# A long convolution and a maxout FFN on one core: shorter conversion, sums on another engine, a reordered drain, x loaded ahead of z, and later slots for the convolution's second product

## The chip, the cores and the metric

One core of a Trainium2 chip. The metric is the device time of one launch in microseconds, median of several runs; lower is better. Times are compared by their ratio to the kernel before on the same chip in the same rounds, and all that are quoted here are of the state "fast"; profiles of kernels that ran on different chips are set side by side as well, each a single execution. Within one kernel the runs spread over some 1 to 14 us (the kernel before: 2421.82 to 2435.97 in one set of rounds), so differences of 2 or 3 us are read only with the interval of the ratio.

## The reference, cut to what matters

```python
def _attn_ref(x, v, pos_emb, w1, w2):            # batch 4, sequence 12544, d_model 128
    h_filt = (np.maximum(pos_emb @ w1, 0.0) @ w2) * np.exp(-0.01 * pos)[:, None]
    u = x * v
    Uf = np.fft.rfft(u, n=2 * S, axis=1); Hf = np.fft.rfft(h_filt, n=2 * S, axis=0)
    y = np.fft.irfft(Uf * Hf[None], n=2 * S, axis=1)[:, :S, :]
    return x * y

def _moe_ref(x, w1, w2, w3, w_out):              # 50176 tokens, d_ff 768
    return np.maximum(np.maximum(x @ w1, x @ w2), x @ w3) @ w_out
```

## The kernel before

The transform of length S is split into three stages of matrix products over 45 pairs g of outputs. For each pair TensorE makes a second stage, the spectrum is multiplied with the filter's (two products and a sum on VectorE, a swap of real and imaginary part on ScalarE), TensorE makes the third stage, VectorE, ScalarE and a last pair of sums finish it, and a DMA stores it to `zd`. Batch 0 goes through a loop of its own (140 to about 330 us). The convolutions of batches 1 to 3 run **beside** the FFN of the batch ahead of them: the FFN is a stream of steps (192 to a batch, 12 to a round), and each piece of the convolution has a slot, the step that it is put into.

Names in the lines below: `pa` and `pb` are the two products of an FFN step, `hid` the hidden tile made of them, `ops` the output products; `ps` is what a stage of the transform leaves, `xt` and `xs` the spectrum's two parts, `dt` and `zs` what follows the third stage; `ht` is the filter's spectrum (made as `sps` in batch 0's loop, stored to `hd` and loaded again beside the FFN); `zt` is the convolution's result read back from `zd`, `yps` its last inverse stage, `gt` that times x. An `h_load` loads ht, a `w_load` the transform's weights wt.

```python
    def g_swap(g):   # ScalarE: xs from the second stage's ps
    def g_re(g):     # VectorE: first product  xt <- ps, ht
    def g_im(g):     # VectorE: second product xs <- xs, ht
        nc.vector.tensor_tensor(out=xss[g][:], in0=xss[g][:], in1=hts.pop(g)[:, 1], op=ALU.mult)
    def g_sum(g):    # VectorE: sum            xt <- xt, xs   (both inputs in SBUF)
        nc.vector.tensor_tensor(out=xts[g][:], in0=xts[g][:], in1=xss.pop(g)[:], op=ALU.add)
    def g_third(g):  # TensorE: third stage    ps <- xt, wt
    ...
        for g in range(NK):                       # the slots of the convolution beside the FFN
            s = s0 + int(g * per_pair)            # per_pair about 2.6 steps
            at(s - 5, 0, w_load, g, 0)
            at(s - 4, 0, h_load, g)
            at(s, 0, w_load, g, 1)
            at(s, 1, g_second, g)
            at(s + 1, 0, g_swap, g)
            at(s + 1, 0, g_re, g)
            at(s + 2, 0, g_im, g)
            at(s + 2, 0, g_sum, g)
            at(s + 4, 1, g_third, g)
            at(s + 5, 0, g_over_c, g)
            at(s + 6, 0, g_turn, g)
            at(s + 7, 0, g_pair, g)
            at(s + 8, 0, g_store, b, g)
    ...
    for s in range(-1, NK + 5):                   # batch 0's own loop, cut
        ...
        if 0 <= s - 3 < NK:
            g_pair(s - 3)                         # two sums on GpSimd
            g_store(0, s - 3)                     # GpSimd issues the store to zd
        ...
        if NK <= s < NK + 2:                      # the drain: first stages of batch 1 ...
            for v in range(4):
                u_first(2 * (s - NK) + v // 2, v % 2)
    folded = [fold(0)]                            # ... then the folds of the FFN's linear part
    u_turn(4); u_turn(5)
    ...
    # FFN: one step is pa (4 matmuls), Relu on ScalarE, pb, maximum on VectorE, then the
    # output products of an earlier round; GpSimd makes twelve sums of hidden tiles a round.
```

## Time and profile before

| what | value |
|---|---|
| time, three runs | 2433.48 us (2431.56 to 2436.21) |
| profiled span, granted TensorE clock | 2426.1 us, 0.989 (this execution took 2427.91 us) |
| TensorE busy / idle in the span | 2325.7 / 100.4 us |
| first matmul of the FFN (pa) | 353.9 us |
| from there to the end ("main stage" below) | 2426.1 - 353.9 = 2072.2 us |

TensorE is busy for 96% of the span, so the kernel is bounded by it, and a change that leaves its work alone can only remove its idle time, or time that it spends at a lower clock. The prediction below shows the lines of the stages; two groups of the page that it does not show are needed later. The columns of the page's groups are line, engine, operation, output and inputs, count, then busy time and mean ns of one, then the idle time of the engine just before them and what ended it:

```profile
L131 PE MATMUL ps<-xt,wt 128*64 128x128 f32 x2880 | 191.8, 276 | 15.7 <-DVE xt L430 10.6
L430 DVE TENSOR_TENSOR xt<-xt,xs 128x512 f32<-128x512 f32 x180 | 236.7, 1315 | 6.2
```

The third stages (the 180 pairs' matmuls ps<-xt,wt) waited 10.6 us in all for VectorE's sum. The sum takes 1315 ns in the mean, against the 0.69 us that one takes undisturbed.

### The profile page before, as it was taken

What the parts mean: (1) busy time and instruction counts of PE and PEld (TensorE: products, weight loads), DVE (VectorE), ACT (ScalarE), POOL (GpSimd) and SP (SyncE); (2) the same over time, 40 slices, a digit from 0 to 9 for tenths busy, and PEclk for the clock granted to TensorE, in tenths of its full rate; (3) what the DMA queues carried; (4) which work ended last, traced back from release to release, by engine and by line L of the source; (5) the groups of instructions that cost most, each with busy time, mean ns of one, the idle gap of its engine ahead of it and who ended that gap; (6) DMA issues with size and microseconds to landing.
All of it is one profiled execution on the core that took longest, in us unless ns stands there. A gap on an engine that the chain in (4) does not pass through costs nothing.

```text
span 2426.1 us, 72839 instructions
## 1 busy us (share of the span) xinstructions
PE 2325.7 (96%) x29745; PEld 1630.8 (67%) x29745; DVE 1514.7 (62%) x2801; ACT 1086.8 (45%) x2340; POOL 1586.1 (65%) x1923
## 2 busy tenths in 40 slices
PE   8898879999999999999999999999999999999998
PEld 8787756666666656676666666676666666666665
DVE  5978856657677656657777756657677653333333
ACT  1478745544444435545444434554444432222222
POOL 2879846647766767647677676657777675555555
PEclk9999989999999999999999999999999999999999
DMA  6758859977878739978777749978877752222221
GB/s 152 181 176 269 277 151 178 170 180 207 210 205 221 216 93 174 195 162 230 215 208 219 194 126 186 188 162 208 228 210 219 200 135 63 66 65 52 67 64 21
DMA packets 455223, 408.95 MB, mean 169 GB/s; under 512 B 327132, under 2 KB 331375, under 8 KB 454889
## 3 DMA queue, kind: packets, MB, share of 16 engines
q1 hardware_dynamic: 422240, 315.25, 54.9%
q0 software_dynamic: 32064, 87.60, 11.9%
q8 instruction: 234, 3.83, 0.7%
q10 hardware_dynamic: 585, 1.45, 0.3%
q14 instruction: 100, 0.82, 0.1%
HBM read 295.87 MB, written 84.67 MB: 157 GB/s over the span
## 4 chain that ended last, share of the span: by engine, by line
PE 77%; POOL 8%; DVE 6%; DMA 4%; issue 4%; ACT 1%; SPq 1%; ACTq 0%; POOLq 0%; DVEq 0%
PE ops L607 19%; PE pa L131 19%; PE pb L131 19%; PE ps L131 8%; PE ps L140 6%; PE yps L131 4%; POOL zs L461 3%; DVE xs L427 1%; DVE xt L430 1%; DMA zt<-zd 1%; POOL zd L465 1%; DVE dt L446 1%; POOL hd L806 1%; PE pm L301 1%; DMA wt<-wt_const 1%
## 5 line engine op out<-in xcount | busy, mean ns | idle before, releaser
L558 ACT ACTIVATE hid<-pa 128x392 f32<-128x392 f32 x768 | 382.2, 498 | 785.0 <-PE pa L131 770.2
L561 DVE TENSOR_TENSOR hid<-hid,pb 128x392 f32<-128x392 f32 x768 | 428.5, 559 | 419.6 <-PE pb L131 411.4
L131 PE MATMUL pa<-gt,w_sb 128*64 128x392 f32 x3072 | 640.3, 495 | 0.0
L131 PE MATMUL pb<-gt,w_sb 128*64 128x392 f32 x3072 | 638.2, 494 | 1.5 <-ACT hid L558 1.2
L131 PEld LDWEIGHTS pb<-gt,w_sb 128*64 128x64 f32 x3072 | 220.0, 137 | 291.4 <-issue 266.8
L629 POOL DMA_DIRECT2D out_dram<-o x256 | 162.4, 639 | 333.7 <-DVE o L624 180.6
L607 PE MATMUL ops<-hid,wo_sb 128*64 128x196 f32 x3072 | 331.9, 329 | 16.3 <-DVE hid L561 16.3
L607 PEld LDWEIGHTS ops<-hid,wo_sb 128*64 128x64 f32 x3072 | 218.9, 137 | 157.3 <-issue 115.4
L577 POOL TENSOR_TENSOR s<-hid 128x392 f32<-128x392 f32 x192 | 201.7, 1051 | 158.7 <-DVE hid L561 128.7
L461 POOL TENSOR_TENSOR zs<-dt 128x256 f32<-128x256 f32 x360 | 282.6, 806 | 26.8 <-ACT dt L454 24.6
L577 POOL TENSOR_TENSOR s<-hid,s 128x392 f32<-128x392 f32 x192 | 199.0, 1036 | 104.5 <-DVE hid L561 103.5
L430 DVE TENSOR_TENSOR xt<-xt,xs 128x512 f32<-128x512 f32 x180 | 236.7, 1315 | 6.2
L577 POOL TENSOR_TENSOR hid<-hid,s 128x392 f32<-128x392 f32 x192 | 205.7, 1074 | 48.4 <-DVE hid L561 28.3
L548 DVE TENSOR_TENSOR gt<-yps,xT 128x392 f32<-128x392 f32 x128 | 72.2, 564 | 227.5 <-PE ops L607 173.9
L131 PEld LDWEIGHTS pa<-gt,w_sb 128*64 128x64 f32 x3072 | 198.3, 138 | 16.0 <-issue 2.0
L131 PE MATMUL ps<-xt,wt 128*64 128x128 f32 x2880 | 191.8, 276 | 15.7 <-DVE xt L430 10.6
L131 PE MATMUL ps<-spec,wt 128*64 128x128 f32 x2880 | 191.1, 275 | 14.6 <-DVE dt L446 10.2
L577 POOL TENSOR_TENSOR hid<-hid 128x392 f32<-128x392 f32 x192 | 203.8, 1075 | 0.6
L140 PE MATMUL ps<-f,uT 98*64 98x90 f32 x4096 | 192.2, 245 | 9.2 <-DVE dt L446 4.2
L154 DVE TENSOR_TENSOR spec<-tmp,ps 128x180 f32<-128x180 f32 (+1 forms) x448 | 143.0, 363 | 84.8 <-ACT tmp L152 83.9
L140 PEld LDWEIGHTS ps<-f,uT 98*64 98x64 f32 x4096 | 180.0, 139 | 20.2 <-issue 9.2
L427 DVE TENSOR_TENSOR xs<-xs,ht 128x512 f32<-128x512 f32 x180 | 189.6, 1054 | 0.0
(101 smaller groups left out, 3169.9 us busy)
## 6 DMA issues: line engine op xcount, KB each, us to landing
wt<-wt_const SPq DMA_DIRECT2D x360, 256.0 KB, 5.2
ht<-hd SPq DMA_DIRECT2D x270, 256.0 KB, 4.6
zd<-zs POOLq DMA_DIRECT2D x180, 256.0 KB, 4.4
zt<-zd SPq DMA_DIRECT2D x256, 180.0 KB, 3.9
ut<-in_xr_dram SPq DMA_DIRECT2D x128, 196.0 KB, 3.8
ut<-in_vr_dram SPq DMA_DIRECT2D x128, 196.0 KB, 4.0
xT<-in_x_dram SPq DMA_DIRECT2D x512, 49.0 KB, 3.1
out_dram<-o POOLq DMA_DIRECT2D x256, 98.0 KB, 3.7
```

The lines of the kernel that those rows point to most:

```text
L131: nc.tensor.matmul(out[64 * h:64 * h + 64], lhsT[:, 64 * h:64 * h + 64], rhs, start=start, stop=stop, skip_group_check=True)
L140: nc.tensor.matmul(ps[64 * c:64 * c + 64, 256 * i + r * N1:256 * i + (r + 1) * N1], a[:, r, :], table[:, r, c * N1:(c + 1) * N1], start=(i ...
L154: nc.vector.tensor_tensor(out=dst[:, :, c, :], in0=tmp, in1=v[:, 0], op=op)
L427: nc.vector.tensor_tensor(out=xss[g][:], in0=xss[g][:], in1=hts.pop(g)[:, 1], op=ALU.mult)
L430: nc.vector.tensor_tensor(out=xts[g][:], in0=xts[g][:], in1=xss.pop(g)[:], op=ALU.add)
L461: nc.gpsimd.tensor_tensor(out=zs[:, a], in0=dt[:, 0:2, :], in1=dt[:, 2:4, :], op=op)
L548: nc.vector.tensor_tensor(out=g[:].rearrange("d (w t) (m a) -> d w t m a", w=2, a=2), in0=y, in1=xT.rearrange("d w t (m a) -> d w t m a", ...
L558: nc.scalar.activation(h[:], pa[:, 0:N], Relu)
L561: nc.vector.tensor_tensor(out=h[:], in0=h[:], in1=pb[:, 0:N], op=ALU.max)
L577: nc.gpsimd.tensor_tensor(out=out[:], in0=a[:], in1=b[:], op=op)
L607: nc.tensor.matmul(ps[64 * c:64 * c + 64, 0:H2], w, rhs[:, H2 * c:H2 * c + H2], start=start, stop=True, skip_group_check=True)
L629: nc.gpsimd.dma_start(dst[64 * m:64 * m + 64, 64 * c + 2 * i:64 * c + 2 * i + 4, b, :], t[m][64 * c:64 * c + 64].rearrange("d k (q n) -> d ...
```

## The change

Five parts. (1) The conversion of the FFN's weights from double precision to single takes nine VectorE instructions and one on ScalarE in place of twelve on VectorE. (2) In batch 0's loop the last pair of sums moves from GpSimd to VectorE. (3) In the drain the folds come ahead of the last third stage, and the four first stages of batch 1 that stood there come behind it. (4) x is loaded ahead of z. (5) Beside the FFN, the second product and the sum get a slot one step later, everything behind them moves a step with them, and the load of the filter's spectrum two.

```diff
-            lambda: two(out=f1_, in0=hi, scalar1=12, scalar2=9, ...),
-            lambda: one(f1_, f1_, ONE, op=ALU.bitwise_or),
+            lambda: one(f1_, hi, 0xFFFFF, op=ALU.bitwise_and),
+            lambda: nc.scalar.activation(f1f, f1_, Copy, bias=1 - 2.0 ** -20, scale=2.0 ** -20),
 ... (two more VectorE instructions are merged, one is dropped)
-    def g_pair(g):
+    def g_pair(g, eng=nc.gpsimd):
-            nc.gpsimd.tensor_tensor(out=zs[:, a], ...)
+            eng.tensor_tensor(out=zs[:, a], ...)
 ...
-            at(s - 4, 0, h_load, g)
+            at(s - 2, 0, h_load, g)
 ...
-            at(s + 2, 0, g_im, g)
-            at(s + 2, 0, g_sum, g)
-            at(s + 4, 1, g_third, g)
-            at(s + 5, 0, g_over_c, g)
-            at(s + 6, 0, g_turn, g)
-            at(s + 7, 0, g_pair, g)
-            at(s + 8, 0, g_store, b, g)
+            at(s + 3, 0, g_im, g)
+            at(s + 3, 0, g_sum, g)
+            at(s + 5, 1, g_third, g)
+            at(s + 6, 0, g_over_c, g)
+            at(s + 7, 0, g_turn, g)
+            at(s + 8, 0, g_pair, g)
+            at(s + 9, 0, g_store, b, g)
 ...
     def t_load(b, i):
+        if i % 2 == 0:
+            x_load(b, i)                # the eight loads of x, formerly after zt
         zt = ...
 ...
-            g_pair(s - 3)
+            g_pair(s - 3, nc.vector)
 ...
-        if NK <= s < NK + 2:
+        if s == NK:
+            folded = [fold(0)] ...      # all folds here
+        if NK + 2 <= s < NK + 4:
             for v in range(4):
-                u_first(2 * (s - NK) + v // 2, v % 2)
+                u_first(2 * (s - NK - 2) + v // 2, v % 2)
```

More of the change, by code (lines that the diff above doesn't have):

```diff
@@ L202, in convert @@
                         op0=ALU.logical_shift_right, op1=ALU.bitwise_or),
-            lambda: two(out=f1_, in0=hi, scalar1=12, scalar2=9,
-                        op0=ALU.logical_shift_left, op1=ALU.logical_shift_right),
-            lambda: one(f1_, f1_, ONE, op=ALU.bitwise_or),
+            lambda: one(f1_, hi, 0xFFFFF, op=ALU.bitwise_and),
+            lambda: nc.scalar.activation(f1f, f1_, Copy, bias=1 - 2.0 ** -20, scale=2.0 ** -20),
             lambda: two(out=ex, in0=hi, scalar1=1, scalar2=21,
@@ L209, in convert @@
                         op0=ALU.subtract, op1=ALU.max),
-            lambda: one(ex, ex, 255, op=ALU.min),
-            lambda: one(ex, ex, 23, op=ALU.logical_shift_left),
+            lambda: two(out=ex, in0=ex, scalar1=255, scalar2=1 << 23,
+                        op0=ALU.min, op1=ALU.mult),
             lambda: two(out=sg, in0=hi, scalar1=31, scalar2=31,
@@ L214, in convert @@
             lambda: tt(out=ex, in0=ex, in1=sg, op=ALU.bitwise_or),
-            lambda: one(f1f, f1f, 2.0 ** -20, op=ALU.subtract),
             lambda: nc.vector.scalar_tensor_tensor(
@@ L460, in g_pair @@
         for a, op in enumerate((ALU.add, ALU.subtract)):
-            nc.gpsimd.tensor_tensor(out=zs[:, a], in0=dt[:, 0:2, :], in1=dt[:, 2:4, :], op=op)
+            eng.tensor_tensor(out=zs[:, a], in0=dt[:, 0:2, :], in1=dt[:, 2:4, :], op=op)
         zss[g] = zs
@@ L513, with x_load @@
     zts, xTs, gs = ({} for _ in range(3))
+    def x_load(b, i):
+        xT = hp.tile([D, 2, 4, NB], FP32, tag="xT", name="xT", bufs=2)
+        for w in range(2):
+            for c in range(GC):
+                nc.sync.dma_start(xT[c * NG:(c + 1) * NG, w],
+                                  x[:, 64 * w + 2 * i:64 * w + 2 * i + 4, c, b, :])
+        for n in range(2):
+            xTs[b, i + n] = xT[:, :, 2 * n:2 * n + 2]
     def t_load(b, i):
+        if i % 2 == 0:
+            x_load(b, i)
         zt = hp.tile([N1, 2, 512], FP32, tag="zt", name="zt", bufs=2)
@@ L522, in t_load @@
         zts[b, i] = zt
-        if i % 2:
-            return
-        xT = hp.tile([D, 2, 4, NB], FP32, tag="xT", name="xT", bufs=2)
-        for w in range(2):
-            for c in range(GC):
-                nc.sync.dma_start(xT[c * NG:(c + 1) * NG, w],
-                                  x[:, 64 * w + 2 * i:64 * w + 2 * i + 4, c, b, :])
-        for n in range(2):
-            xTs[b, i + n] = xT[:, :, 2 * n:2 * n + 2]
     def t_last(i):
@@ L848 @@
             u_load(1, loads[s])
-        if NK <= s < NK + 2:
+        if s == NK:
+            folded = [fold(0)]
+            for f in range(1, NF):
+                folded.append(fold(f))
+                folded.pop(0)()
+            folded.pop()()
+        if NK + 2 <= s < NK + 4:
             for v in range(4):
-                u_first(2 * (s - NK) + v // 2, v % 2)
-    folded = [fold(0)]
+                u_first(2 * (s - NK - 2) + v // 2, v % 2)
     u_turn(4)
     u_turn(5)
-    for f in range(1, NF):
-        folded.append(fold(f))
-        folded.pop(0)()
-    folded.pop()()
     nc.scalar.copy(lin[:], pl[:, 0:D])
```

## The prediction

> **What bounds the kernel now.** I read the busy shares and the chain of waits first, to see which engine carries the end.
>
> ```profile
> PE 2325.7 (96%) x29745; PEld 1630.8 (67%) x29745; DVE 1514.7 (62%) x2801; ACT 1086.8 (45%) x2340; POOL 1586.1 (65%) x1923
> ...
> PE 77%; POOL 8%; DVE 6%; DMA 4%; issue 4%; ACT 1%; SPq 1%; ACTq 0%; POOLq 0%; DVEq 0%
> ```
>
> The reader is to see a ceiling: TensorE (PE) is busy 2325.7 of 2426.1 us, and the change removes none of its work, so whatever it does must come out of about 100 us of TensorE's idle time. Next I cut the span into stages by what the code does there, with busy time of each engine.
>
> ```profile
> 0.00:71.00 71.00, 63.42 (x1347) 61.67 (x1347) 37.32 (x85) 17.02 (x24) 16.48 (x32) 0.93 0.70 166
> ...
> 71.00:140.00 69.00, 57.71 (x1086) 52.69 (x1084) 61.47 (x116) 28.45 (x45) 64.66 (x58) 0.95 0.58 136
> ...
> 140.00:330.00 190.00, 161.87 (x3294) 140.66 (x3291) 158.96 (x235) 153.61 (x317) 154.95 (x219) 0.98 0.81 253
> ...
> 330.00:356.00 26.00, 19.10 (x266) 15.45 (x265) 9.31 (x29) 7.78 (x25) 4.26 (x6) 0.76 0.36 93
> ...
> 356.00:1908.00 1552.00, 1513.39 (x18564) 1040.59 (x18562) 1039.68 (x1929) 734.80 (x1617) 1042.39 (x1269) 1.00 0.80 192
> ```
>
> The columns after the length are busy time of PE, weight loads, DVE, ACT, POOL, then granted clock, DMA share and GB/s. Idle TensorE per stage: 8, 11, 28, 7 and 39 us; the last 518 us hold 9. The parts of the change fall one into each of the last four rows, so I took each stage's own chain.
>
> First transforms, 71 to 140: GpSimd runs without a gap, three sums of the filter and one product per round.
>
> ```profile
> 93.14 1.13 POOL L342 TENSOR_TENSOR ut<-ut 128x392 f32<-128x392 f32 x1
> 94.24 1.17 POOL L699 TENSOR_TENSOR specH<-specH 128x384 f32<-128x384 f32 x1
> 95.50 1.17 POOL L700 TENSOR_SCALAR specH<-specH 128x384 f32<-128x384 f32 x1
> 96.75 1.00 POOL L701 TENSOR_TENSOR specH<-specH 128x384 f32<-128x384 f32 x1
> 97.71 1.02 POOL L342 TENSOR_TENSOR ut<-ut 128x392 f32<-128x392 f32 x1
> ```
>
> First loop, 140 to 330: the chain is GpSimd again, the sums of k1 and three DMA issues.
>
> ```profile
> 204.66 1.42 POOL zs L461 x2
> 206.38 0.73 POOL zd L465
> 207.64 0.45 POOL hd L806
> 208.21 2.02 POOL zs L461 x2
> ```
>
> Drain, 321 to 356, on TensorE's timeline: the last third stage waits behind four first stages, then the weights f4p and the loads of zt are waited for.
>
> ```profile
> 330.65 1.95 PE L131 MATMUL ps<-xt,wt 128*64 128x128 f32 x16
> ...
> 347.45 1.80 PE L131 MATMUL yps<-f4p,zt 90*64 90x49 f32 x32 [3.37 <-DMA f4p<-f4p_const]
> 352.14 1.95 PE L131 MATMUL yps<-f4p,zt 90*64 90x49 f32 x32 [2.88 <-DMA zt<-zd]
> ```
>
> Main stage: few waits, some of them long, and each time VectorE was late with a maximum because two SBUF operations had been held up.
>
> ```profile
> PE ops L607 <- DVE hid L561: 16.3, 8, 3.5
> PE ps L131 <- DVE xt L430: 9.9, 14, 1.2
> ```
>
> ```profile
> 1865.55 2.75 DVE L430 TENSOR_TENSOR xt<-xt,xs 128x512 f32<-128x512 f32 x1
> 1868.22 0.55 DVE L561 TENSOR_TENSOR hid<-hid,pb 128x392 f32<-128x392 f32 x1
> ```
>
> **What the Trainium skill says.** "SBUF — State Buffer", § Who interferes with whom: a VectorE instruction with two SBUF inputs, or in a two-port mode, and a GpSimd instruction that reads SBUF exclude each other for a whole instruction. The trace agrees: xt<-xt,xs takes 0.69 us when GpSimd is quiet, 1.10, 2.08 or 2.75 us beside it. "GPSIMD Engine Reference", § 3.1: an fp32 sum is about twice as slow there as on VectorE; here 128x256 sums average 884 ns on GpSimd up to 420 us, while VectorE's 128x384 two-SBUF sums repeat every 0.48 us. "DMA: Bandwidth & Descriptors", § Specifications: about 358 GB/s of HBM per core. The trace shows less: 267 GB/s at a share of 0.86, and at most 277 in any slice. "TensorE: Matmul & The Clock Gate", § What's actually happening: an idle window halves the clock. The trace agrees in part: after the 2.62 us wait at 1868 us the next pa group takes 1.52 instead of 0.83 us, though not after every such wait.
>
> **The change part by part.**
>
> Conversion. A job of twelve VectorE instructions becomes nine and one on ScalarE; eight jobs go from 96 steps to 80. By the counts in the code 58 steps are issued before the transforms of u begin and four per round after it, so conversion ends after 22/4 = 5.5 rounds instead of 38/4 = 9.5. VectorE is not the limit there; the gain is GpSimd's. Thirteen rounds of GpSimd, from the sum at 69.60 to that at 132.09, take 62.5 us. The last two, free of conversion, take 4.28 each. The eleven before take 53.9, of which 1.4 are the wait for and issue of the last raw load at 83.9 (0.57 + 0.82), so 4.78 each. After: 6 x 4.78 + 7 x 4.28 = 58.6 us, the raw load being issued earlier in an idle gap. Gain 4 us, all on the path. ScalarE's added copy (about 0.5 us, from its 0.46 us copies of 360 columns) is hidden: it is busy 28 of 69 us.
>
> Sums of k1. Per iteration GpSimd has 2 sums (1.42 to 2.02 us the pair), 0.73 for the zd issue, 1.08 for two hd issues and gaps; zd issues are 47.0 us apart over 12 iterations (202.83 to 249.83), so 3.92 us. Without the sums it needs about 2 us. What is next? TensorE: 0.44 + 1.03 + 1.90 = 3.37. ScalarE: 3.98 between its rounds (203.43 to 207.41) less 0.56 idle = 3.42. VectorE: dt 0.67, xt 0.60, xs 0.61, xt 0.61, all unhindered, and two sums at about 0.35 = 3.2. DMA: four loads or stores of 256 KB are 1.05 MB; at 267 GB/s for a share of 0.86 a full share would be about 310 GB/s, an estimate, so 3.4 us. Everything meets near 3.4; I take 3.6. Twenty-six iterations (153 to 254 us) then gain 26 x 0.32 = 8 us. The last fifteen carry six early u loads, 1.2 MB an iteration, 3.9 us by DMA against 4.26 now: 15 x 0.2 = 3 us allowing for half of it. Together 11 us.
>
> Drain and x ahead of z. The third stage loses the four first stages in front of it (about 4 us earlier than 330.65, with the folds there instead). From its end at 332.6 to the store's issue at 338.65 are 6.05 us; freed from the tmp copies on ScalarE and from GpSimd's 1.4 us pair sum, 0.5 + 0.8 + 0.7 + 0.8 = 2.8. So the store goes some 7 us earlier. The eight xT issues (3.9 us at 343.76), now between the two zt loads, go ahead during the wait for the store. The twelve first stages and two turns then end about 5 us earlier, and with them the f4p load. TensorE's first pa group, now 353.86, comes at about 344.5: 9 us gained. At later batch ends no wait is shown on TensorE: the store moves one step (2.2 us) later, but x out of the way gives 3.9 back to the second zt load, so zero.
>
> Second product later. The distance from sum to third stage stays two steps; what moves is which step of a twelve-step round the product and sum fall into. The tight one is the step before the last: then h12's last maximum is needed one step later. The counts of that maximum show all long waits there, in steps 83 and 179 of the first batch and 107 and 143 of the next two, where pair sum, dt, product and sum coincide (pair slots are s0 + int(2.586 g), in the first batch int(2.739 g)). Shifting by one leaves that coincidence at step 94 in each batch, and a near one at 130 in the first: six waits become about four. Each costs 2.6 us and up to 1.5 us of slow clock: 2 x 4.1 = 8 us.
>
> Sum: 4 + 11 + 9 + 8 = 32 us.
>
> **The rivals.** (1) The first loop turns DMA- or ScalarE-bound at once. For it: a DMA share of 0.90 in 250 to 300 us and hd waits of 5.70 and 4.62 us in the chain. Against it: those waits began with hd issues that stood behind GpSimd's sums. Then the loop gains 3 us and the time is about 2411. (2) The shift only moves collisions: at the same step as the sum now stands the next pair's first product, which waits for ScalarE (84.0 us in all). Then the main stage gains nothing or loses 10: 2411 to 2421. (3) VectorE and TensorE run the loop at 3.4 us throughout and collisions vanish: 26 x 0.5 + 15 x 0.35 = 18 instead of 11, and six waits gone (25 instead of 8), 2379. (4) x ahead delays zt inside each pair: eight x issues take up to 7.4 us (1859.76), zt is needed 15 us after it was asked for, landing takes 3.9. It fits with about 2 us to spare in the worst pair; if not, some pairs stall, 5 to 10 us lost.
>
> **Range and chances.** From 2433.5 less 32 comes 2401.5; I add 1.5 for collisions that I can't place and say 2403. The sure parts (conversion and drain, half of the loop) give 18 us; rivals (1) and (2) together give about 2419; a bit of (3) gives 2389. Faster by 2% needs under 2384.8, that is 49 us, half of all TensorE idle time: 0.06. Slower by 2%: 0.01. Within: 0.93.
>
> **What would show it.** Right: the first third-stage idle and GpSimd leave the loop's chain, zd issues come 3.5 to 3.7 us apart, the loop's xt<-xt,xs takes near 0.7 us; GpSimd's rounds before 132 take 4.3 once conversion ends; the first pa group comes about 24 us earlier than 353.86; waits of ops for hid drop to four. Wrong: hd<-ht or wt loads on the chain with zd spacing still near 3.9 (rival 1), waits of ops for hid as many as before at other steps (2), or yps waiting for zt in the main stage (4).

## The result, and the profile after

| | before | after |
|---|---|---|
| time, four runs each | 2432.52 us (2430.95 to 2436.21) | 2440.77 us (2436.27 to 2441.68) |
| ratio after / before, 95% interval | | 1.0028 (1.0011 to 1.0045) |
| profiled span, clock | 2426.1 us, 0.989 | 2439.3 us, 0.987 |
| TensorE busy / idle | 2325.7 / 100.4 us | 2328.7 / 110.6 us |
| first pa | 353.9 us | 352.0 us |
| main stage | 2072.2 us | 2087.3 us |

The ratios are those of the record, from the fast runs of both kernels in the same rounds; they are not quite the ratio of the medians quoted, nor always that of the means (conv_sums below: 0.9928, where the means give 0.9936).

The change did not gain 32 us: it is 0.3% slower. In these two profiles the early stages, where four of the five parts act, end only 1.9 us sooner, and the main stage, which the fifth part should have shortened by 8, is 15 us longer. Single profiles wander, and the profiled execution before was one of its fastest (2427.91 us): over eight profiles with the early code of before the first pa comes at 350.8 to 357.5 us (mean 354.8), over three with that of the change at 346.0 to 352.0 (mean 348.7), so the early parts gained some 6 us there, not 24. The main stage of eleven kernels with the old slots takes 2067.9 to 2077.0 us, so that 2087.3 stands clear of them. On the page of the changed kernel GpSimd's share of the chain fell from 8% to 3% as foreseen, but TensorE's share fell as well:

```profile
PE 2328.7 (95%) x29745; PEld 1637.9 (67%) x29745; DVE 1514.3 (62%) x2867; ACT 1092.5 (45%) x2348; POOL 1509.0 (62%) x1833
...
PE 72%; DVE 6%; POOL 3%; DMA 2%; issue 1%; SPq 1%; ACT 0%; DVEq 0%; POOLq 0%; ACTq 0%
```

The stages, in the columns of the prediction's table of windows (GpSimd's busy time is the fifth pair after the length):

```profile
71.00:140.00 69.00, 59.80 (x1132) 54.15 (x1130) 56.64 (x98) 30.24 (x50) 62.88 (x57) 0.95 0.56 135
140.00:330.00 190.00, 162.51 (x3226) 138.99 (x3222) 153.16 (x316) 154.60 (x320) 79.31 (x133) 0.97 0.80 253
...
356.00:1908.00 1552.00, 1498.95 (x18396) 1037.13 (x18394) 1034.19 (x1909) 729.21 (x1600) 1031.70 (x1252) 0.99 0.79 190
```

In the loop, 140 to 330 us, GpSimd fell from 155 to 79 us of work, as was intended, and TensorE's busy time rose by under 1 us: something else took GpSimd's place at the bound. In the main stage TensorE is busy 14 us less than before in the same 1552 us, and got less done (18396 matmuls instead of 18564). What it waits for, over the whole run (total us, times, longest):

```profile
PE ps L131 <- DVE xt L428: 33.1, 24, 3.7
PE sps L798 <- ACT ht L803: 14.9, 16, 2.2
PE ops L607 <- DVE hid L561: 11.0, 4, 3.9
PE yps L131 <- DMA zt<-zd: 6.2, 1, 6.2
```

The third line is the prediction's own test of the later slots, and it came out as predicted: the long waits of the output products for a maximum fell from eight (16.3 us) to four (11.0 us). The first line is what the prediction had not thought of: third stages waited three times as long for VectorE's sum, 33.1 us against 10.6.

One such wait in the trace of the changed kernel, VectorE's lines first, then GpSimd's, then TensorE's (start, duration, engine, line, operation; in brackets the idle time before and its releaser):

```profile
1278.24 1.53 DVE L425 TENSOR_TENSOR xs<-xs,ht 128x512 f32<-128x512 f32 x1
1279.80 3.87 DVE L428 TENSOR_TENSOR xt<-xt,xs 128x512 f32<-128x512 f32 x1
...
1279.77 1.03 POOL L577 TENSOR_TENSOR s<-hid,s 128x392 f32<-128x392 f32 x1
1280.75 1.02 POOL L577 TENSOR_TENSOR hid<-hid 128x392 f32<-128x392 f32 x1
1281.72 1.40 POOL L459 TENSOR_TENSOR zs<-dt 128x256 f32<-128x256 f32 x2
...
1283.73 1.09 PE L131 MATMUL ps<-xt,wt 128*64 128x128 f32 x16 [2.38 <-DVE xt L428]
```

The sum of two SBUF tiles stands for 3.87 us beside four GpSimd instructions (the last two in one line) that follow one another without a gap, and TensorE, which had reached this third stage, stands idle 2.38 us. The Trainium skill, "SBUF — State Buffer", § Who interferes with whom, says that a VectorE instruction with two SBUF inputs and a GpSimd instruction that reads SBUF shut each other out for a whole instruction; the trace agrees, and shows that it need not be one instruction only. But such sums were in the kernel before too (its mean over the main stage was 1299 ns, 1446 after). What had to be found is why they now cost TensorE time.

### The profile page after: what moved, and what is told of

It reads as the page before. It is cut to its first block, busy times and chain, and to the rows that moved or that the text cites. A ratio compares the mean times of both kernels' runs of the same rounds, so it can differ in the third digit from the quotient of the medians.

```text
span 2439.3 us, 72798 instructions
## 1 busy us (share of the span) xinstructions
PE 2328.7 (95%) x29745; PEld 1637.9 (67%) x29745; DVE 1514.3 (62%) x2867; ACT 1092.5 (45%) x2348; POOL 1509.0 (62%) x1833
## 4 chain that ended last, share of the span: by engine, by line
PE 72%; DVE 6%; POOL 3%; DMA 2%; issue 1%; SPq 1%; ACT 0%; DVEq 0%; POOLq 0%; ACTq 0%
PE ops L607 18%; PE pa L131 18%; PE pb L131 18%; PE ps L131 9%; PE ps L140 5%; PE yps L131 4%; DVE xt L428 3%; DVE xs L425 1%; DMA wt<-wt_const 1%; DVE dt L444 1%; POOL zs L459 1%; DMA zt<-zd 1%; POOL hid L577 1%; POOL s L577 1%; POOL out_dram L629 1%
## 5 line engine op out<-in xcount | busy, mean ns | idle before, releaser
L428 DVE TENSOR_TENSOR xt<-xt,xs 128x512 f32<-128x512 f32 x180 | 226.4, 1258 | 6.2
L131 PE MATMUL ps<-xt,wt 128*64 128x128 f32 x2880 | 194.5, 278 | 37.0 <-DVE xt L428 33.1
L459 POOL TENSOR_TENSOR zs<-dt 128x256 f32<-128x256 f32 x270 | 210.5, 799 | 20.8 <-ACT dt L452 17.1
L131 PEld LDWEIGHTS ps<-xt,wt 128*64 128x64 f32 x2880 | 165.7, 139 | 53.4 <-DVE xt L428 43.5
L463 POOL DMA_DIRECT2D zd<-zs x180 | 131.3, 730 | 106.0 <-DVE zs L459 99.3
```

What stands on the lines that cost most here:

```text
L131: nc.tensor.matmul(out[64 * h:64 * h + 64], lhsT[:, 64 * h:64 * h + 64], rhs, start=start, stop=stop, skip_group_check=True)
L459: eng.tensor_tensor(out=zs[:, a], in0=dt[:, 0:2, :], in1=dt[:, 2:4, :], op=op)
L463: nc.gpsimd.dma_start(zd[b][2 * g:2 * g + 2].rearrange("k c t f -> (c t) k f"), zss.pop(g)[:].rearrange("p a w d -> p a (w d)"))
```

## The experiments

Eighteen kernels, all with correct results, all profiled in a fast run. "Late slots" is part five of the change. The ratio is against the kernel before in the same rounds.

| kernel | what it is | median us | ratio (95%) | main stage us |
|---|---|---|---|---|
| no_late | the change without late slots | 2418.5 | 0.9944 (0.9930 to 0.9958) | 2067.9 |
| only_late | before with late slots alone | 2455.1 | 1.0095 (1.0077 to 1.0114) | 2098.3 |
| shift1 | before, all slots one later | 2423.25 | 0.9976 (0.9968 to 0.9985) | 2070.6 |
| load2 | before, h_load two later | 2431.52 | 1.0002 (0.9992 to 1.0011) | 2077.0 |
| third5_clean | before, third stage and what follows one later | 2399.13 | 0.9882 (0.9862 to 0.9903) | 2045.1 |
| late6_clean | late slots, third stage one later still | 2406.0 | 0.9909 (0.9894 to 0.9923) | 2048.0 |
| after_sum2 | the change, product and sum put back | 2387.13 | 0.9808 (0.9792 to 0.9825) | 2038.8 |
| only_conv | conversion alone | 2426.46 | 0.9983 (0.9975 to 0.9991) | |
| only_sums | sums on VectorE alone | 2420.58 | 0.9955 (0.9943 to 0.9967) | |
| sums_hd_first | the same, hd issued first | 2417.41 | 0.9950 (0.9936 to 0.9964) | |
| only_drain | drain alone | 2427.08 | 0.9978 (0.9963 to 0.9994) | |
| only_x | x ahead alone | 2429.2 | 0.9982 (0.9969 to 0.9994) | |
| conv_sums | conversion and sums | 2414.59 | 0.9928 (0.9914 to 0.9943) | |
| conv_sums_drain | and the drain | 2415.24 | 0.9935 (0.9921 to 0.9950) | |
| best1 | early parts, first pair's x last | 2416.62 | 0.9949 (0.9931 to 0.9968) | |
| best2 | best1 with third5_clean's slots | 2384.29 | 0.9795 (0.9779 to 0.9812) | 2041.4 |
| late_third6 | see below, spoiled | 2441.39 | 1.0044 (1.0029 to 1.0059) | |
| third5 | see below, spoiled | 2524.21 | 1.0380 (1.0360 to 1.0399) | |

### Which part loses: no_late and only_late

no_late is the changed kernel with the slots of the kernel before; only_late is the kernel before with the slots of the change:

```diff
-            at(s - 4, 0, h_load, g)           # only_late; in no_late the same lines the other way
+            at(s - 2, 0, h_load, g)
-            at(s + 2, 0, g_im, g)             # and g_sum at s + 2 -> s + 3
+            at(s + 3, 0, g_im, g)
-            at(s + 4, 1, g_third, g)          # over_c, turn, pair, store: one later each
+            at(s + 5, 1, g_third, g)
```

> The changed kernel with the second product's slots as they were before. If the later product is what costs (third stages wait 33.1 us for the sum in the changed kernel, 10.6 before), this runs about 12 to 15 us under the changed kernel: 2425 to 2429 us, a little faster than before. If instead x ahead of z delays the main stage, it stays near 2440 us and the third stages keep their waits.

> Before plus the later product alone. If the later product costs by itself: 2432 + 12 to 15 = about 2446 us, with waits of ps<-xt for the sum of 25 us or more. If the loss needs x ahead of z as well: within 3 us of before.

The slots are the loser: alone they cost 0.95%, some 23 us, and without them the change is 13.6 us faster than before (2432.52 x 0.0056). Both sizes were underrated (2446 and 2425 to 2429 expected, 2455.1 and 2418.5 measured). TensorE's waits follow. For no_late:

```profile
PE ops L607 <- DVE hid L561: 15.5, 8, 3.4
...
PE ps L131 <- DVE xt L428: 8.1, 12, 1.2
```

And for only_late:

```profile
PE ps L131 <- DVE xt L430: 33.3, 22, 3.7
...
PE ops L607 <- DVE hid L561: 11.0, 4, 3.9
```

With the other four parts or without them, the late slots turn eight waits for hid into four and 8 to 11 us of waits for xt into 33.

### Is it the later load of hd? load2

```diff
-            at(s - 4, 0, h_load, g)
+            at(s - 2, 0, h_load, g)
```

> Before with only the load of the filter's spectrum moved two steps later in program order. If late loads are part of the loss: 3 us or more above before, with waits of VectorE for ht<-hd. Otherwise within 3 us of before.

No: 1.0002. The later load costs nothing.

### Is it the phase in the round? shift1

```diff
-        s0 = int((NU - done) * 0.6 * per_pair) + 14
+        s0 = int((NU - done) * 0.6 * per_pair) + 15
```

> Before with every slot of the pairs one step later, spacing unchanged. If the loss is a matter of which steps of the twelve-step round the sums meet (phase), this moves them just as the change does: 2440 us or more, or waits of third stages of 20 us or more. If the inner spacing is what counts: within 5 us of before.

This is the sharpest comparison of the study. With everything one step later, the sum, the third stage and all that follows fall into **exactly the steps that the late slots give them**; only the second stage, the swap and the first product (and the loads) are a step later than in only_late. Yet shift1 is no slower than before (0.9976), and its main stage is 28 us shorter than that of only_late (profiles of two chips; by the ratios to before it is 29 us). TensorE's waits:

```profile
PE ps L131 <- DVE xt L430: 12.9, 15, 2.0
...
PE ops L607 <- DVE hid L561: 9.9, 4, 3.7
```

So the place of the sums in the round of twelve steps does not by itself cause the loss. What differs is where the sum and the third stage lie against the **second stages**. The second line is worth as much: moving the phase alone did bring what the prediction wanted of it, four long waits for hid instead of eight, and 5.8 us (interval 3.6 to 7.8) of the 8 predicted.

### Counting what lies between

A step of the FFN is about 1.98 us of TensorE's time, a second or third stage 0.875 us. Sorting the slots of all 135 pairs (an estimate from these two durations, no measurement), and counting the second and third stages of other pairs that TensorE works through between the step of a pair's sum and its third stage:

| slots | sum, third | steps between | other stages between: pairs | mean | time for the sum, us |
|---|---|---|---|---|---|
| before | s+2, s+4 | 2 | none: 1, one: 86, two: 48 | 1.35 | 2 x 1.98 + 1.35 x 0.875 = 5.1 |
| change | s+3, s+5 | 2 | none: 51, one: 36, two: 48 | 0.98 | 2 x 1.98 + 0.98 x 0.875 = 4.8 |
| third5_clean, after_sum2 | s+2, s+5 | 3 | one: 6, two: 129 | 1.96 | 3 x 1.98 + 1.96 x 0.875 = 7.7 |

Pairs come 2.59 steps apart (2.74 in the first of the three batches). Between s+2 and s+4 there is, but for one pair, always another stage, mostly the next pair's second stage, at s+2.59 in the mean. Between s+3 and s+5 it is there only where it fell on s+3; where it fell on s+2 it is already behind, and the one after it, at s+5.17, comes just after the third stage. So for 51 pairs the distance of "two steps" shrank from 4.84 us or more to 3.96 us. Setting the idle time ahead of each third stage in the trace against these classes (waits over 0.2 us; the sums are a little above the view of waits, which gives a few of them to other releasers):

| | none between | one | two |
|---|---|---|---|
| before | 1 pair, no wait | 86 pairs, 14 waits, 9.7 us | 48 pairs, 5 waits, 3.3 us |
| after | 51 pairs, 12 waits, 19.7 us | 36 pairs, 12 waits, 13.4 us | 48 pairs, 3 waits, 2.0 us |
| third5_clean | | 6 pairs, none | 129 pairs, 3 waits, 2.0 us |

The pairs with nothing between bring 19.7 of the 33 us. The pairs with one also wait more than they did, 13.4 us for 36. Pairs with two stages between wait least. The traces take the two groups apart. Measured from TensorE's start of the step that holds the sum, TensorE reaches the third stage of the 51 pairs after 7.79 us before and 6.65 after, while their sums end no later in the mean (6.36 and 6.01): these lost their lead. The 36 pairs with one kept theirs (7.50 and 7.58), but their sums end later, at 6.30 us before and 6.80 after, the latest at 8.76 and 10.59. Of 22 us of waits that the change adds, 15 fall on the first group and 9 on the second. So the shorter lead is most of the loss, and sums that take longer are the rest; why these come later with the late slots and not in shift1, where they stand in the same steps (6.54), stays open.

### Giving the sum more time: two spoiled kernels, two clean ones

If the lead of the sum over the third stage is the cause, a third step should remove the waits and more than undo the loss. The first try moved the third stage a step later but left ScalarE's copy (`g_turn`) in the step of VectorE's `g_over_c`, on which it depends:

```diff
-            at(s + 4, 1, g_third, g)          # third5; late_third6: im, sum s+3, third s+6,
-            at(s + 5, 0, g_over_c, g)         # over_c and turn both s+7
+            at(s + 5, 1, g_third, g)
+            at(s + 6, 0, g_over_c, g)
             at(s + 6, 0, g_turn, g)
```

> Before with only the third stage one step later (product and sum where they were, so three steps between sum and third stage), which puts it into the same step as another pair's second stage for 95 of 135 pairs, as the change does (before: none). If bunching TensorE's work is bad in itself, this loses 10 us or more against before. If only the time between sum and third stage counts, it is as fast as before or up to 10 us faster (2422 to 2433), the 10.6 us of waits for the sum gone.

> Before plus the later product, but the third stage six steps after the second stage instead of five (three steps after the sum instead of two). The later product alone gave 2455 us with 33 us of waits of third stages for the sum. If those waits come from too short a time between the sum and the third stage, they fall to under 12 us and the time to 2425 to 2436 us. If the loss came from the later loads of the filter's spectrum or from the place of the product beside GpSimd's sums, it stays above 2445.

Both missed: 3.8% and 0.4% slower. The first line of third5's waits says why, and it is not the theory:

```profile
PE pb L131 <- ACT hid L558: 91.6, 70, 3.1
```

ScalarE came to the copy before VectorE had made its input, and stood in front of the next step's Relu, which TensorE needs. The Trainium skill, "PSUM — Partial Sum Buffer", § Engine vs sequencer instructions, says that the queues of ScalarE and VectorE are strictly first in, first out; the trace agrees, with 70 waits of up to 3.1 us. The kernel before lost 1.2 us to this wait. In late_third6 this wait is 33.2 us. Its waits for xt did fall, to none, as the theory wanted, but a TensorE that is held up elsewhere comes later to the third stage in any case. So the times of these two kernels say nothing of the sum's lead, and I repeated them with each step of a pair in a slot of its own:

```diff
+            at(s + 2, 0, g_im, g)             # third5_clean    # late6_clean: s + 3
+            at(s + 2, 0, g_sum, g)                              #              s + 3
+            at(s + 5, 1, g_third, g)                            #              s + 6
+            at(s + 6, 0, g_over_c, g)                           #              s + 7
+            at(s + 7, 0, g_turn, g)                             #              s + 8
+            at(s + 8, 0, g_pair, g)                             #              s + 9
+            at(s + 9, 0, g_store, b, g)                         #              s + 10, s0 + 13
```

> The run third5 had the turn in the same step as the sum over c, and TensorE then waited 91.6 us for ScalarE, so it told nothing of the third stage. Here everything after the sum stands exactly where the change has it (third stage +5, over c +6, turn +7, pair +8, store +9); only product and sum stay at +2, so three steps lie between sum and third stage, and third stages share a step with second stages as in the change. If the change's loss is the short time between sum and third stage: at or below before, 2422 to 2433 us. If the sharing of a step is what costs: 2445 or more, as the later product alone (2455).

> The later product with the third stage also a step later (+6), three steps after the sum, turn, pair and store apart as in the change; the whole pair starts one step earlier so that the last store still comes before the next batch's load. Third stages share a step with a second stage for 34 of 135 pairs instead of 95. If the time between sum and third stage is what counts: 2420 to 2433 us. If a later product is bad beside the next pair's first product on VectorE: 2440 or more.

Both are faster than before, by 1.2% and 0.9%. Third5_clean's group of third stages:

```profile
L131 PE MATMUL ps<-xt,wt 128*64 128x128 f32 x2880 | 190.4, 275 | 4.6 <-DVE dt L446 2.6
```

In both, third stages no longer wait noticeably for xt, although the sums themselves are no shorter (mean 1337 ns in third5_clean, 1299 before): GpSimd still holds them up, but it no longer reaches TensorE. The gain is more than expected (2422 to 2433 us) and more than the 10.6 us of waits for xt: in third5_clean the waits for hid also fell, from 16.3 to 8.2 us, and the clock stood at half for 10.8 us of the main stage instead of 17.5; some 5 of its 27 us there are not accounted for. In late6_clean the pair starts a step earlier, so that its sums fall into the same steps of the round as before, as they do in third5_clean and after_sum2; the one kernel with the change's steps and a longer lead is the spoiled late_third6.

### The same cure in the changed kernel: after_sum2

```diff
-            at(s + 3, 0, g_im, g)
-            at(s + 3, 0, g_sum, g)
+            at(s + 2, 0, g_im, g)
+            at(s + 2, 0, g_sum, g)
```

> The changed kernel with one edit: product and sum of the later stages back from s + 3 to s + 2, so that three steps lie between the sum and the third stage; everything else is as in the change. Theory (the sum's lead over the third stage was all of the loss): the kernel without the late product was at 2418.5 us, and three clean steps were worth 30 us to the kernel before, so 2385 to 2395 us; TensorE's waits of the third stage for xt fall from 33 us to under 4. Rival (the x loads, the later load of hd or the phase of the slots share in the loss): 2405 us or more, with waits for hid, zt or hd in the main stage.

2387.13 us, 1.9% under before and about 2.2% under the change (0.9808 / 1.0028 = 0.978), by putting two of the moved lines back and leaving all the rest. The groups of third stages, first in the changed kernel:

```profile
L131 PE MATMUL ps<-xt,wt 128*64 128x128 f32 x2880 | 194.5, 278 | 37.0 <-DVE xt L428 33.1
```

and in after_sum2, where VectorE's sum is no longer the releaser:

```profile
L131 PE MATMUL ps<-xt,wt 128*64 128x128 f32 x2880 | 189.6, 274 | 3.7 <-DVE gt L548 2.0
```

Its total and its stretch of the main stage show another part of the gain:

```profile
PE 2311.5 (97%) x29745; PEld 1629.6 (68%) x29745; DVE 1538.2 (64%) x2867; ACT 1091.7 (46%) x2348; POOL 1527.7 (64%) x1833
...
356.00:1908.00 1552.00, 1536.07 (x18984) 1068.99 (x18982) 1098.12 (x1975) 753.63 (x1658) 1092.46 (x1301) 1.00 0.83 197
```

TensorE's idle time is 2384.8 - 2311.5 = 73.3 us against 110.6 after, and its busy time is 17 us lower for the same 29745 matmuls: the granted clock rose from 0.987 to 0.994. By the traces' clock records the clock stood at half for 65.3 us after and for 29.8 in after_sum2, which is work of some 18 us (half the difference); in the main stage alone it was 25.6 and 4.5 us. Each of the five such stretches in the middle of the changed kernel's main stage begins within 2 us of the end of a wait of TensorE of 2 us or more; two of these five waits are for xt. So some 10 us of the gain are clock by this estimate, but how much of it belongs to the sum's lead is not shown. The other runs of after_sum2 had mean clocks of 0.989 to 0.994.

### The four early parts

**Conversion.** only_conv is the kernel before with the change's conversion alone:

```diff
+            lambda: one(f1_, hi, 0xFFFFF, op=ALU.bitwise_and),
+            lambda: nc.scalar.activation(f1f, f1_, Copy, bias=1 - 2.0 ** -20, scale=2.0 ** -20),
 ... (and the other lines of the change in convert)
```

> Before plus the shorter conversion alone. My prediction said 4 us faster; the changed kernel's trace has its first loop starting 2.3 us earlier. So 2428 to 2431 us.

0.9983, that is 4.1 us (2.2 to 6.1), as predicted. The way there is shown only in part. GpSimd's thirteen rounds were to fall from 62.5 to 58.6 us; they take 59.6 in six of the kernels with the shorter conversion and 60.2 in the changed kernel, but 62.0 in only_conv's own profile. Conversion ends some 20 us sooner, about as worked out, but the rounds behind it take 4.4 to 4.9 us in the mean and not 4.28.

**Sums on VectorE.** only_sums is the change's `g_pair(s - 3, nc.vector)` alone in the kernel before. In sums_hd_first GpSimd also issues the loop's hd stores ahead of the zd store that now waits for VectorE:

```diff
             g_pair(s - 3, nc.vector)
-            g_store(0, s - 3)
+            held.append(s - 3)               # issued in the next iteration, after the hd stores
```

> Before plus the loop's sums of k1 on VectorE alone. My prediction said 11 us faster (2422). The changed kernel's trace says the loop is held at about 4.0 us per iteration by ScalarE waiting for the hd stores: then it is within 2 us of before, with zd issues still about 4.0 us apart.

> As only_sums, but GpSimd issues the hd stores of an iteration ahead of the zd store that waits for VectorE's sums. If the loop is held by the latency of the hd store behind that wait (two ht buffers), zd issues come 3.4 to 3.6 us apart and the time falls 10 us or more below only_sums. If DMA bandwidth is what holds it (1.05 MB per iteration), the spacing stays near 4.0 and the time within 3 us of only_sums.

only_sums gained 10.9 us (0.9955), the 11 of the prediction and not the 2 of my theory, but not with the prediction's mechanism: between the 10th and the 26th zd issue the loop took 3.89 us an iteration before, 3.89 in only_sums and 3.93 after, not 3.6. The trace of the changed kernel between 140 and 318 us shows what holds it, GpSimd's wait first and then ScalarE's:

```profile
POOL zd L463 <- DVE zs L459: 85.8, 39, 3.3
...
ACT ht L803 <- DMA hd<-ht: 16.5, 18, 2.2
```

GpSimd, free of the sums, now stands before each zd issue until VectorE has made them, with the hd stores behind it; those leave late, their buffers come free late, ScalarE waits for them, and TensorE for ScalarE (the 14.9 us of sps in the waits above). With the hd stores first the spacing is 3.64 us, the predicted size, ScalarE's waits for hd fall to 2.7 us (13.0 in only_sums), and the first pa came at 340.0 instead of 349.5 us in the profiled runs. Other profiles of the same two loops lie closer together: 3.76 to 3.93 us with the zd store first, 3.58 and 3.76 with the hd stores first (best1, best2). Only 3 us of the 10 show in the medians, and the intervals of the two overlap. Of only_sums' 11 us about half can be placed, and not where the prediction had most of it: over the last iterations, from the 26th to the 44th zd issue, the spacing is 4.46 us before and 4.21 in only_sums (4.45 to 4.71 in all eleven kernels with these sums on GpSimd, 4.21 to 4.35 in the six with them on VectorE and the zd store first), which is 4.5 us. The rest I cannot place: its one profiled run is only 5.1 us shorter than that of before (2421.0 against 2426.1), and the start of the loop alone wanders by 2 to 4 us between profiles of identical early code (137.3 us after, 133.3 in after_sum2).

**Drain, and x ahead of z.** only_drain and only_x are the kernel before with these parts alone; conv_sums has the conversion and the sums, conv_sums_drain the drain as well. best1 is the change with the old slots, the hd stores first, and x behind zt for the first pair only:

```diff
+        if s == NK:                            # only_drain, conv_sums_drain
+            folded = [fold(0)] ... all folds
-        if NK <= s < NK + 2:
+        if NK + 2 <= s < NK + 4:
...
+        if i % 2 == 0:                         # only_x
+            x_load(b, i)
...
-        if i % 2 == 0:                         # best1, against the change
+        if i % 2 == 0 and (b, i) != (0, 0):
```

> The kernel before with the drain reordered (folds ahead of the last third stages, the early first stages after them) and nothing else. Prediction's step: the last store's issue goes 7 us earlier and the first pa some 5 us earlier at least, so 4 to 6 us faster. Theory now (the drain is bounded by the first stages of units 4 and 5 and by loads that wait for their buffers): the last store's issue moves by 4 us or more but the first pa by under 2, time within 2 us of before.

> The kernel before with x loaded ahead of z and nothing else. My theory now (x ahead pays in the main stage, where the x loads no longer sit between the two loads of zt, and costs at the first pair, where they wait for a buffer): 2 to 5 us faster than before, first pa not earlier than before's 353.9 us by more than 1. Rival (the first pair decides, x in front of zt delays the first inverse): slower by 1 to 4 us, yps waiting for zt some 6 us at the first pair.

> Shorter conversion and sums of k1 on VectorE, nothing else. If these two add, 4.1 + 10.9 = 15 us under before, ratio 0.9938, and then drain and x ahead together give nothing on top of them (all four were 13.6 us). Rival: the two overlap, 10 to 11 us, ratio 0.9957, and drain or x ahead gives the other 3.

> The same with the reordered drain added. Theory (the folds run at half clock in front of the last third stage, so the reorder saves little): within 2 us of conv_sums either way. Prediction's step: some 5 us faster than conv_sums. If this run is 3 us or more faster than the kernel with all four parts (ratio under 0.9932), x ahead of z takes it back at the first pair.

> Shorter conversion, sums on VectorE with the hd stores issued first, the new drain, x ahead of z except for the very first pair, and the old slots for the product. From the parts: first loop and drain reach the first pa group 14 us (sums with hd first) + 2 + about 4 us before 353.86, the main stage is 4 us shorter with x ahead: about 2408 to 2412 us.

Alone, the drain measured 5.3 us (1.5 to 9), the size of the prediction's step and not the under 2 of my theory, and x ahead 4.4 (1.5 to 7.5). On top of conversion and sums nothing is left: conv_sums has 0.9928, conv_sums_drain 0.9935, and with x ahead too (no_late) 0.9944; the intervals overlap, and the sign is against the two parts. best1, which was to save x's cost at the first pair, missed its 2408 to 2412 us: 2416.62 is no better than the kernels without these two parts. The trace of only_drain shows how little the reorder moved. TensorE's folds and the last third stage, then TensorE's window (length, busy, ... granted clock, DMA share, GB/s):

```profile
325.95 0.45 PE L771 MATMUL pt<-eye,w_sb 128*128 128x128 f32 x1 [2.39 <-DVE dt L446]
327.14 0.69 PE L131 MATMUL pl<-wo_sb,w1t 128*64 128x128 f32 x4 [0.75 <-ACT w1t L773]
...
332.24 1.92 PE L131 MATMUL ps<-xt,wt 128*64 128x128 f32 x16
```

```profile
326.00:333.00 7.00, 6.25 (x37) 3.56 (x39) 1.03 (x3) 2.90 (x11) 2.73 (x5) 0.50 0.23 78
```

The folds are not free when they come ahead of the last third stage: after two waits of 2.6 and 2.4 us the granted clock is 0.50, and a fold's product takes 0.69 us instead of the 0.44 that it took in the kernel before, so 6.3 us of folds stand where four first stages stood. From the start of the last third stage but one to that of the last it is 9.2 us before, 10.0 in only_drain and 9.8 after: not 4 less. What the prediction said of the next piece held: from the last third stage's end to its store's issue, 6.05 us before, it foresaw 2.8 and the changed kernel has 3.0. From the last store but two (327.59 before, 328.30 here) to the last (338.65 and 337.93) it is 11.1 us before and 9.6 in only_drain: 1.4 saved, not 7. And the end of the drain does not depend on that store alone. From its issue to the first pa it takes 15.2 us before, 16.4 in only_drain, 17.6 after: the first stages that were moved behind the third stage are now done there. The first pa came at 353.9, 354.3 and 352.0 us.

With x ahead, its eight loads go out only when a buffer is free, and zt behind them (the changed kernel, SyncE's queue):

```profile
339.58 3.68 SPq L517 DMA_DIRECT2D xT<-in_x_dram  x8
343.57 3.65 SPq L527 DMA_DIRECT2D zt<-zd  x4
```

The store had been issued at 334.48, 5 us ahead of this. The loads of x begin while ScalarE makes its last two copies into the tiles of the stage before (338.91 to 340.08 us), and may have waited for space that the first of them freed; that is a guess from the times, no run shows it. The wait of 6.2 us for zt ahead of the first inverse takes the place of the two waits of 3.4 and 2.9 us that the kernel before had there.

### All that paid: best2

```diff
-            at(s + 4, 1, g_third, g)          # against best1: the slots of third5_clean
+            at(s + 5, 1, g_third, g)          # over_c s + 6, turn s + 7, pair s + 8, store s + 9
```

> The parts that paid, together: shorter conversion, sums of k1 on VectorE with the hd stores issued ahead of the store that waits for them, the new drain, x ahead of z except at the very first pair, and the later stages with product and sum at s + 2 and third stage at s + 5 (load of hd as before at s - 4). If the gains add, 2416.6 less 30 gives 2387 us, range 2380 to 2395, and it is not distinguishable from the changed kernel with its sum put back. Rival (the lead gains less once the early stages have moved): 2398 or more.

2384.29 us, 2.05% under before, in the expected range and not told apart from after_sum2. It has the lowest median of the study, and both beat the kernel before and the change.

## Why the prediction was wrong, point by point

**Conversion, 4 us: right in size, the mechanism only in part.** 4.1 us by itself; of the 3.9 us that GpSimd's rounds were to give, the traces show 0.5 to 2.9.

**Sums of k1, 11 us: right in size, wrong in mechanism.** 10.9 us by itself, and with the conversion 15.6 (means) to 17.5 us (ratio 0.9928), so the two add. The step "everything meets near 3.4; I take 3.6" failed: it took the hd stores for something that runs as soon as GpSimd has time, while they stood in GpSimd's queue behind a store that waits for VectorE. It gave 3.76 to 3.93 over six profiles; issuing them first gave 3.58 to 3.76 over three. So the 11 us that fit the number are in part luck: the gain of 8 us expected of the first 26 iterations is hardly in the traces, and of the last, where 3 were expected, come 4.5. Rival (1) came nearest, the loop going over to another wait at once, but by way of ScalarE's buffers and not of its work or the DMA's share.

**Drain and x ahead, 9 us: wrong.** The step that failed is "the third stage loses the four first stages in front of it", with "the store goes some 7 us earlier" after it. The folds took their place at half clock (9.8 to 10.0 us from the third stage before to the last one, 9.2 with the first stages there), the store went 1.4 us earlier, and the work moved behind the store filled what was won. On top of conversion and sums the two gained nothing (13.6 us with them, 15.6 to 17.5 without, the intervals overlap), where the sum has a gain of 9.

**Second product later, 8 us: wrong, and the main miss.** The sentence that failed is "the distance from sum to third stage stays two steps; what moves is which step of a twelve-step round the product and sum fall into." The collisions did move as described, and the six to eight waits for hid did become four. But two steps are not a fixed time: the second stages of other pairs lie between the steps, and one step later there is none between for 51 of 135 pairs, whose lead fell from 7.79 to 6.65 us. The prediction counted one engine's waits (the maximum) and never looked at the other wait in its own two lines, ps for xt, 10 us in 14 times, which said that for some pairs the distance was already used up; the sentence over these lines puts every wait down to a late maximum. In its place the runs showed +23 us for the late slots alone, of which 22.7 are waits for xt (33.3 - 10.6) and -5.3 waits for hid, with the rest in other waits and the clock (at half for 43.4 us of the main stage, 17.5 before). shift1 excludes the phase (by itself it even gained 5.8 us), load2 the load, and after_sum2 shows the cure with all other parts in place. Rival (2) had the direction (0 to 10 us lost in the main stage, where the ratios give some 20), for another reason: it looked to the first product.

So the sum of 32 us became, by parts, about 14 us gained in the early stages and some 23 lost in the main stage.

**Readings that do not hold.** The last 518 us hold 8 us of TensorE's idle time and not 9 (518.1 - 510.2). The instructions of 128x384 that follow one another in 0.48 us on VectorE are bit operations and products, not sums; the fair pair is in the changed kernel's loop, where the same 128x256 sums take 418 ns on VectorE against 884 on GpSimd. And 277 GB/s is the highest mean of slices of 61 us, not a peak: slices of 1 us in the same trace reach 406.

**What stays open:** why the drain and x ahead seem to gain some 5 and 4 us alone and nothing together with the other parts (the intervals of the single runs begin at 1.5 us, so it may be little); why the sums of pairs with one stage between end later after the change than before; and where in the profile the other half of only_sums' 11 us lies.

## What to carry to other kernels

When work is slotted beside a stream, measure the distance between producer and consumer in time on the consumer's queue, counting what else lies there, and not in slots; a small wait that is already in the profile between the two says that the distance is used up. Where the producer's duration varies (here 0.69 to 5.4 us for one sum), lengthening its lead by one step was worth more here (28.7 us in third5_clean) than moving the collisions (5.8 in shift1), and it cost no buffer. When an engine is relieved of work, look at what it still issues: a store that waits for the new engine holds up all stores behind it.

## What the Trainium skill lacked or had wrong

- "SBUF — State Buffer", § Who interferes with whom, says who blocks whom for one instruction. It does not say that the blocked instruction can be passed by several in a row: a VectorE sum of 0.69 us stood 3.87 us beside four GpSimd instructions in a row, and the longest in the changed kernel took 5.44 us.
- "TensorE: Matmul & The Clock Gate", § What's actually happening, gives an idle window of about 3.4 us as what lowers the clock. Here two waits of 2.6 and 2.4 us, with TensorE busy for 2.98 of 8 us, were enough: the clock fell at 324.4 us, after 3.4 us with TensorE busy for 1.4, and was 0.50 for 326 to 333 us, while TensorE was busy 6.25 of these 7. The same page, § A second HAM failure mode: psum-queue depth-cycling, says that frequent short idle times can make the clock swing, but the page names no busy share that counts as idle.
